# DMA issues pinned in program order, new queue times in the planner, and the output weights moved into the pattern buffers

## The chip, the cores and the metric

The kernel runs on one core of a Trainium2 chip. The metric is the time of one execution on the device, in microseconds, as the median of several executions. A profiled execution is one more execution of the same program, taken with the hardware profiler; its span runs from its first to its last instruction.

## What is computed

Two independent attention problems, A and B, share the launch; their outputs stand side by side in the last dimension. Both have 2048 rows, a model width of 512, and 32 heads of 16 channels.

```python
def _B_ref(x, wqkv, wo):
    q, k, v = ...                      # x @ wqkv, split in heads
    scores = einsum('bhqd,bhkd->bhqk', q, k) * Dh ** (-0.5)
    o = einsum('bhqk,bhkd->bhqd', softmax(scores), v)
    return o.reshape(B, S, D) @ wo

def _A_ref(x, wq, wk, wv, wo, beta):   # N = 4 segments of L = 512 rows
    for s in range(N):
        a_dot = softmax(qs @ ks^T * scale + causal mask) @ vs
        a_mem = (phi(qs) @ M) / (phi(qs) @ z + 1e-06)   # memory of earlier segments
        o = g * a_mem + (1.0 - g) * a_dot               # g = sigmoid(beta), per head
        M, z = M + phi(ks)^T @ vs, z + sum(phi(ks))     # phi(t) = t + 1 or exp(t)
    return o.reshape(B, S, D) @ wo
```

Problem B has full attention over 2048 keys, so it has by far the larger number of exponentials: 32 heads x 2048 x 2048.

## The kernel before

**Units and quads.** Heads are handled in groups. A unit is a problem, a chunk of 512 queries (`ch`), a row tile `rt` of eight heads and a half `e` of them, so four heads at a time. For one block of 128 keys (`kb`), a unit needs four score blocks of 128 x 512, one for each head of the four, made by four matmuls that use 32 rows of the array each. The exponentials of such a block go one of two ways.

- *The ScalarE way.* `scores` (L861) takes score blocks from a stream, alternately three and two at a time, into one of two PSUM tiles `s_ps`; ScalarE turns the tile of 1536 or 1024 columns into `pT` in one ACTIVATE (L882).
- *The VectorE way.* `v_scores` (L935) puts a score block into a PSUM tile `v_ps`. VectorE turns it into a half-precision bit pattern by a multiply and an add into an integer (L955, four of them for four heads). Three more integer additions over the whole pattern (L971, `v_rung`) give three shifted copies; the sum of the four approximates the exponential. All four patterns are then multiplied with V. The tiles of these patterns have the tag `vx` and `VBUFS = 11` buffers of 4 KB per partition.

Products with V are accumulated in a PSUM tile `acc` by matmuls with 32 columns each, four for a `pT` block, sixteen for a block that went the VectorE way. `zeros` matmuls (`zero`, L1103) add nothing to `acc`; they keep TensorE active.

**What sets the order.** The order is made while the program is built, by a planner written out in the kernel (L1142 to L1191). It keeps its own clocks `T["pe"]`, `T["act"]`, `T["dve"]`, `T["pool"]` and `T["sp"]`, adds constants for each operation, and picks at each step the next score tile, a V product, a chore or a filler. Chores are everything else: projections, `phi`, the memory matmuls, normalization and output projections. A chore has a due place in the stream of score blocks, and may have an `after` time or an `ok` condition. Whether a block goes the VectorE way is decided in `v_scores` and `v_pick` (L910) from VectorE's planned backlog and from `vlive`, the count of `vx` buffers in use: a new block is begun only while `vlive` is at most `VBUFS - 2`, and a copy only while it is below `VBUFS`. Compute instructions are pinned: `pin` (L96) keeps them in the order in which they were written, engine by engine. DMA issues are not pinned.

**The DMA queue.** Nearly all DMAs are issued from SyncE (SP), in one order: input weights, transposed loads of x (`load_xT`, L231), the output weights (`load_wo`, L226, called at L489 and L490), and later, in the stream, four transposing DMAs for each `phk` (L330, the transposed `phi(k)`), four for each later chunk of x, and the stores of the output (L454). The planner's `T["sp"]` is moved on by `on_sp` with 1.3 us for a transposed load of x, 1.45 us (`SPTRANS`) for a `phk` transpose and 0.55 us for a store; a projection of a newly loaded chunk is let go 3.5 us after its last issue.

**Buffers at the start.** Two weight tiles of B and three chunks of B's x occupy five of the eleven `vx` buffers at first and give them up when the last projection that reads them has been written. The two output weights have their own places in the pool `big`.

**The end.** After the last tile of the stream, L1209 to L1257 finish the last unit: transposition, reciprocal, normalization, the last output matmuls and the last stores.

A branch with an exact computation (L1367) follows; it isn't entered.

Of the kernel before, what the change touches and what calls it, by code (L numbers as in the profile page):

```python
# [13 lines left out]
BF16 = mybir.dt.bfloat16  # L14
# [6 lines left out]
P = 128  # L21
H = 32
DH = 16
D = H * DH
NRT = 4
NSEG = 4
W = 512
# [30 lines left out]
VALONE = 1.4  # L58
POOLMIN = 99
SPLOADS = 38.0  # L60
SPTRANS = 1.45
POOLTT = 1.2
POOLSLACK = -99.0
POOLWITH = 1.2
# [9 lines left out]
def kernel(  # L74
# [74 lines left out]
    def palloc(pool, shape, name):  # L149
        t = pool.tile(shape, F32, name=name, tag="misc")  # L150
        if live[0]:
            i = min(range(3), key=lambda i: slots[i])
            assert slots[i] < 1e9
            slots[i] = 1e9
            slot_of[id(t)] = (i, t)
        return t

    def on_sp(us, ready):
        T["sp"] = max(T["sp"], ready) + us
# [29 lines left out]
    rsum = const.tile([P, 64, 16], F32, name="rsum")  # L189

    def load_beta():
        nc.sync.dma_start(out=beta_a[:], in_=A_beta.partition_broadcast(P))

    def spread_beta():
        for j in range(4):
# [20 lines left out]
    def load_w(homes, name):  # L216

        t = [p.tile([P, 4, D], BF16, name=f"w_{name}", tag=tag, bufs=bufs) for p, tag, bufs in homes]
        srcs = ([B_wqkv[:, i * D:(i + 1) * D] for i in range(3)] if name == "b" else [A_wq, A_wk, A_wv])

        def load(eng, i, lo=0, hi=D):
            eng.dma_start(out=t[i][:, :, lo:hi],
                          in_=srcs[i][:, lo:hi].rearrange("(cc p) n -> p cc n", p=P))
        return t, load

    def load_wo(pool, name, eng):  # L226
        t = pool.tile([P, NRT, D], BF16, name=f"wo_{name}", tag=f"wo_{name}")
        eng.dma_start(out=t[:], in_=wos[name].rearrange("(rt p) n -> p rt n", p=P))
        return t

    def load_xT(pool, name, ch, tag, bufs):  # L231
        t = pool.tile([P, 4, W], BF16, name=f"xT_{name}", tag=tag, bufs=bufs)
        for cc in range(4):
            nc.sync.dma_start_transpose(t[:, cc, :], xs[name][ch * W:(ch + 1) * W, cc * P:(cc + 1) * P])
        return t

    def v_heads(v, kb):
# [85 lines left out]
    def do_phik(wk, k, out, then=None):  # L323

        pk = wk.tile([P, W], BF16, name="phkT", tag="phkT")

        def move():
            ph = out["ph"] = wk.tile([P, 4, P], BF16, name="phk", tag="phk", bufs=2)
            for kb in range(4):
                nc.sync.dma_start_transpose(ph[:, kb, :], pk[:, kb * P:(kb + 1) * P])  # L330
            on_sp(4 * SPTRANS, T["dve"] + 0.1)
            if then is not None:
                then()
        phase1(wk, k, pk[:], move)
        yield
# [105 lines left out]
        pin(nc.vector.tensor_reduce(okm, okt, axis=AX.X, op=ALU.min))  # L441

    def do_out(mp, wk, name, ot, wo, ch, sb, then=None):
        ps = palloc(mp, [P, D], "o_ps")
        for rt in range(NRT):
            mm(ps[:], ot[:, rt, sb * P:(sb + 1) * P], wo[:, rt, :], start=(rt == 0), stop=(rt == NRT - 1))
            if rt < NRT - 1:
                yield

        def evac():  # L450
            osb = wk.tile([P, D], BF16, name="osb", tag="osb", bufs=3)
            pin(nc.vector.tensor_copy(osb[:], ps[:]))  # L452
            r0 = ch * W + sb * P
            nc.sync.dma_start(out=out2[r0:r0 + P, col0[name]:col0[name] + D], in_=osb[:])  # L454
            on_sp(0.55, T["dve"] + 0.1)
        later(0.69, evac, ps)
        if then is not None:
            then()
# [6 lines left out]
    with ExitStack() as ms:  # L465
# [20 lines left out]
        ld(nc.sync, 0)  # L486
        ld(nc.sync, 2)
        xTB += [load_xT(wk, "b", ch, "vx", VBUFS) for ch in range(1, 4)]
        woA = load_wo(big, "a", nc.sync)  # L489
        woB = load_wo(big, "b", nc.sync)  # L490

        zeros = wk.tile([P, 1, P], BF16, name="zeros")
        nc.gpsimd.memset(zeros[:], 0.0)
# [60 lines left out]
        def seg_chores(s, rt):  # L554
            d = pos0["a", s, rt]

            def k():
                kA[s, rt] = wk.tile([P, W], BF16, name="kA", tag=f"kA{rt}")
                yield from do_k(mp, wA, xTA[s], rt, kA[s, rt][:], ("k", "a", s, rt))

            def q():
                qA[s, rt] = wk.tile([P, 2, W], BF16, name="qA", tag=f"qA{rt}")
                if s > 0:
                    phq[s, rt] = wk.tile([P, W], BF16, name="phq", tag=f"phq{rt}")
                yield from do_q(mp, wk, wA, xTA[s], rt, qA[s, rt], phq[s, rt][:] if s > 0 else None, ("q", "a", s, rt), s == 0)

            def v(kb):
                yield from do_v(mp, wA, xTA[s], kb, v_heads(vA[s], kb)[:, :, 0:DH], ("v", "a", s, kb))

            def part(g):  # L570
                yield from g
                nproj[s] = nproj.get(s, 0) + 1

            def project():
                rel = T["sp"] + 3.5
                if (s, rt) != (0, 0):
                    chore(d - LEAD, part(k()), 4, after=rel if s else ARRIVE["w1" if rt == 1 else "wk"],
                          key=("k", "a", s, rt), ok=lambda: s == 0 or ("phk", s - 1, rt) in seen)
                    chore(d - LEAD, part(q()), 4, after=rel if s else ARRIVE["w1" if rt == 1 else "wq"],
                          key=("q", "a", s, rt))  # L580
                if rt == 0:
                    for kb in range(4):
                        chore(d + 1 + 0.3 * kb, part(v(kb)), 4, after=rel if s else ARRIVE["wv"])

            def load():
                if s > 0:
                    xTA[s] = load_xT(wk, "a", s, "xTA", 1)
                    on_sp(4 * 1.3, T["pe"])
                vA[s] = wk.tile([P, 4, VROW], BF16, name="vA", tag="vA", bufs=2)
                v_ones(vA[s], 4)  # L590
                project()
                return
                yield
            if rt == 0:
                chore(d - 18, load(), 1, slot=False,
                      ok=lambda: (s < 1 or nproj.get(s - 1, 0) == 12) and (s < 2 or nmem.get(s - 2, 0) == 4))
            else:
                project()
# [34 lines left out]
        def bq_chores(ch, rt):  # L633
            qB[ch, rt] = wk.tile([P, 2, W], BF16, name="qB", tag=f"qB{rt}")

            def q():
                yield from do_q(mp, wk, wB, xTB[ch], rt, qB[ch, rt], None, ("q", "b", ch, rt))
                if rt == NRT - 1 and ch < NSEG - 1:
                    chore(pos0["b", ch, rt] - LEAD - 1.0, again(), 1, slot=False, ok=lambda: left_b[0] == 0)

            def again():
                xTB[ch + 1] = load_xT(wk, "b", ch + 1, "xTB0", 1)
                on_sp(4 * 1.3, T["pe"])
                xat[ch + 1] = T["sp"] + 3.5
                return
                yield
            chore(pos0["b", ch, rt] - LEAD - 1.5, q(), after=ARRIVE["wvb"], key=("q", "b", ch, rt),
                  ok=lambda: xat.get(ch, 1e9) < T["pe"])

        def b_kv_chores():  # L650
# [21 lines left out]
            for sb in range(S // P):  # L672
                chore(pos0["b", 0, 0] - 0.5 + 0.9 * sb, counted("v", sb // 4, g=do_v(
                    mp, wB, xTB[sb // 4], sb % 4, v_heads(VB, sb)[:, :, 0:DH], ("v", "b", sb))),
                      after=max(ARRIVE["wvb"], ARRIVE["xb"][sb // 4]))

        held.update(pk=0, ph=0)
        vlive, npool = [5], [0]

# [352 lines left out]
        def finish(u, st):  # L1032
            name, ch, rt = u["name"], u["ch"], u["rt"]
            if (name, ch) not in OT:
                assert sum(outs.get(k, 4) > 0 for k in OT) < 3
                OT[(name, ch)] = wk.tile([P, NRT, W], BF16, name=f"OT_{name}", tag="OT", bufs=3)
            ot = OT[(name, ch)]
            yield from fin_pair(wk, st, name, rt, u["sums"], ot[:, rt, :])
            if rt == NRT - 1:
                outs[name, ch] = 4  # L1040

                def gone():
                    outs[name, ch] -= 1
                at = place()
                for sb in range(4):
                    chore(at + 8 + 4 * sb, do_out(mp, wk, name, ot, woA if name == "a" else woB, ch, sb, gone))

        def v_key(q):
            u = q["u"]
# [164 lines left out]
        def partial(sb, t):  # L1214
            ps[sb] = t
            for rt in range(NRT - 1):
                mm(t, ot[:, rt, sb * P:(sb + 1) * P], woB[:, rt, :], start=(rt == 0), stop=False,
                   skip_group_check=True)
        last = [ps_s.tile([P, BANKS[(NT + i) % 2], 512], F32, name="l_ps", tag=f"s{(NT + i) % 2}") for i in range(1)]
        left = [(3, lambda: mp.tile([P, D], F32, name="l_ps3", tag="misc")[:]),  # L1220
# [14 lines left out]
        for sb in range(4):  # L1235
            pin(nc.vector.transpose(ot[:, NRT - 1, sb * P:(sb + 1) * P],
                                    tN[:, 4 * sb:4 * sb + 4, :].rearrange("p c d -> p (c d)")))
            mm(ps[sb], ot[:, NRT - 1, sb * P:(sb + 1) * P], woB[:, NRT - 1, :], start=False, stop=True,
               skip_group_check=True)
            if sb == 1:  # L1240
                fps = ps_a.tile([P, W], F32, name="f_ps", tag="misc")
# [18 lines left out]
    def exact_problem(name):  # L1260
        is_a = name == "a"
        with ExitStack() as es:
# [17 lines left out]
            w, ld = load_w([(big, f"w{i}", 1) for i in range(3)], name)  # L1280
            for i in (1, 0, 2):
                ld(nc.sync, i)
            wo = load_wo(big, name, nc.sync)
            xT = [load_xT(big, name, ch, f"xT{ch}", 1) for ch in range(4)]
            K = big.tile([P, NRT, S], BF16, name="K")
            Q = big.tile([P, NRT, 2, S], BF16, name="Q")
# [114 lines left out]
```

## Time and profile before

| | |
|---|---|
| median of 5 runs | 902.3 us (896.31 to 904.59) |
| the profiled execution's own time | 897.77 us |
| its span, first to last instruction | 896.0 us |
| ACT busy | 870.9 us (97%) |
| PE busy, with 417 filler matmuls | 865.7 us (97%) |
| DVE busy | 787.9 us (88%) |
| POOL busy | 154.2 us (17%) |
| mean granted TensorE clock | 0.995 |

Around the span lie 897.77 - 896.0 = 1.8 us. PE is TensorE, ACT ScalarE, DVE VectorE, POOL GpSimd and SP SyncE; PEld are weight loads, which overlap matmuls. A group's line gives the code line, engine, operation, the tile written and the tile read, the count, then busy time, the mean duration of one in ns, and the idle time ahead of it with what ended most of that. All matmuls are recorded at L117, so they are told apart by their tiles. Two matmuls or two ACTIVATEs in a row overlap in the records, so a group's busy time is less than count times mean.

### The profile page before, as it was taken

The page shows a single profiled execution, that of the slowest core. Times are in us where ns is not written, and L with a number is a line of the kernel's source. Part 1 is how long each engine was busy: PE and PEld are TensorE (multiplying, and loading weights), DVE is VectorE, ACT ScalarE, POOL GpSimd, SP SyncE. Part 2 cuts the span into 40 slices and gives each one's busy share as a digit, 9 for nine tenths or more (in the row PEclk, how much of TensorE's full clock was granted, in tenths as well). Part 3 has the DMA queues.
Part 4 walks back from the last instruction along what each step waited for, and adds up shares of the span by engine and source line. Part 5 has one row for each costly group of instructions (what it writes and reads, how often), then busy time and mean ns, then how long its engine had stood idle before and what let it go on. Part 6 is the DMA issues. An engine that isn't in the chain of part 4 may idle for free.

```text
span 896.0 us, 18896 instructions
## 1 busy us (share of the span) xinstructions
PE 865.7 (97%) x7649; PEld 260.2 (29%) x7649; DVE 787.9 (88%) x1348; ACT 870.9 (97%) x781; POOL 154.2 (17%) x332
## 2 busy tenths in 40 slices
PE   9999999999999999999999999999999999999996
PEld 3322222322322222222222323322232222222222
DVE  4786689888799998989889998999999998899996
ACT  6999999999999999999999999999999999999995
POOL 5710311311203022030210304002030300000000
PEclk9999999999999999999999999999999999999998
DMA  9600001100001110000000110000000000000000
GB/s 200 134 10 12 18 8 30 27 6 1 7 1 43 32 28 8 1 1 7 2 7 1 42 31 8 1 1 1 2 1 1 13 30 8 1 2 1 1 2 28
DMA packets 42800, 17.04 MB, mean 19 GB/s; under 512 B 34512, under 2 KB 42704, under 8 KB 42704
## 3 DMA queue, kind: packets, MB, share of 16 engines
q1 hardware_dynamic: 41360, 15.23, 7.4%
q8 instruction: 61, 1.00, 0.5%
q10 hardware_dynamic: 1344, 0.52, 0.2%
q14 instruction: 35, 0.29, 0.1%
HBM read 4.20 MB, written 4.19 MB: 9 GB/s over the span
## 4 chain that ended last, share of the span: by engine, by line
PE 43%; ACT 35%; issue 14%; DVE 5%; POOL 2%; ACTq 0%; DVEq 0%; POOLq 0%
ACT pT L882 34%; PE acc L117 19%; PE s_ps L117 11%; PE v_ps L117 6%; PE k_ps L117 2%; PE o_ps L117 2%; POOL pT L892 1%; DVE vx L955 1%; ACT ex L299 1%; DVE vx L971 1%; PE q_ps L117 1%; PE pre L117 1%; DVE tT L374 1%; DVE qc L272 0%; POOL qB L274 0%
## 5 line engine op out<-in xcount | busy, mean ns | idle before, releaser
L882 ACT ACTIVATE pT<-s_ps 128x1536 bf16<-128x1536 f32 x751 | 858.7, 1281 | 6.9 <-PE s_ps L117 4.6
L955 DVE TENSOR_SCALAR vx<-v_ps 128x512 uint16<-128x512 f32 x492 | 321.5, 683 | 28.4 <-PE v_ps L117 23.9
L117 PE MATMUL s_ps<-qB,KB 32*128 32x512 bf16 x1556 | 251.8, 383 | 10.8 <-ACT pT L882 7.7
L971 DVE TENSOR_SCALAR vx<-vx 128x2048 uint16<-128x2048 uint16 x369 | 242.2, 687 | 2.1 <-PE acc L117 0.8
L117 PE MATMUL acc<-vx,VB 128*32 128x512 f16 x1968 | 178.0, 385 | 1.0 <-DVE vx L955 0.7
L117 PE MATMUL v_ps<-qB,KB 32*128 32x512 bf16 x492 | 174.5, 382 | 1.5 <-DVE KB L253 0.5
L892 POOL TENSOR_SCALAR_AFFINE_SELECT pT<-pT 128x256 bf16<-128x256 bf16 (+2 forms) x240 | 104.6, 467 | 358.3 <-ACT pT L882 357.4
L117 PEld LDWEIGHTS <-KB 32*128 32x128 bf16 x2048 | 84.7, 91 | 245.6 <-issue 238.9
L117 PE MATMUL acc<-pT,VB 128*32 128x512 bf16 x1556 | 150.9, 387 | 0.3 <-DVE tT L374 0.3
L117 PE MATMUL acc<-zeros 128*128 128x512 bf16 x397 | 134.8, 387 | 0.0
L117 PEld LDWEIGHTS <-VB 128*32 128x32 bf16 x3524 | 73.6, 94 | 155.5 <-issue 144.1
L117 PEld LDWEIGHTS <-zeros 128*128 128x128 bf16 x417 | 34.2, 98 | 86.2 <-issue 80.3
L117 PE MATMUL s_ps<-qA,kA 32*128 32x128 bf16 (+3 forms) x512 | 51.4, 299 | 4.8 <-ACT pT L882 2.8
L374 DVE STREAM_TRANSPOSE tT<-acc 128x512 f32<-128x512 f32 x64 | 44.5, 700 | 12.5 <-PE acc L117 12.4
L274 POOL TENSOR_SCALAR qA<-qc,par 128x512 bf16<-128x512 bf16 x24 | 17.3, 733 | 174.8 <-DVE qc L272 174.8
L117 PE MATMUL acc<-pT,vA 128*32 128x256 bf16 (+3 forms) x512 | 32.1, 309 | 1.4 <-DVE vx L955 1.3
L117 PEld LDWEIGHTS <-kA 32*128 32x128 bf16 x512 | 17.7, 91 | 43.9 <-issue 40.9
L274 POOL TENSOR_SCALAR qB<-qc,par 128x512 bf16<-128x512 bf16 x32 | 22.6, 718 | 19.2 <-DVE qc L272 19.2
L272 DVE CAST qc<-q_ps 128x512 bf16<-128x512 f32 x28 | 19.2, 685 | 6.5 <-PE q_ps L117 5.8
L452 DVE CAST osb<-o_ps 128x512 bf16<-128x512 f32 x28 | 19.2, 684 | 5.8 <-PE o_ps L117 5.7
L408 POOL TENSOR_TENSOR tN<-tT,rsum 128x512 bf16<-128x512 f32 x1 | 1.4, 1367 | 130.9 <-DVE rsum L397 130.9
L117 PE MATMUL k_ps<-xT_b,w_b 128*128 128x512 bf16 x64 | 19.3, 383 | 0.4 <-DVE vx L955 0.2
(93 smaller groups left out, 430.7 us busy)
## 6 DMA issues: line engine op xcount, KB each, us to landing
out_dram<-osb SPq DMA_DIRECT2D x30, 128.0 KB, 1.7
w_b<-in_B_wqkv_dram SPq DMA_DIRECT2D x3, 512.0 KB, 5.1
phk<-phkT SPq DMA_TRANSPOSE x48, 2.4
w_a<-in_A_wv_dram SPq DMA_DIRECT2D x1, 512.0 KB, 4.1
wo_a<-in_A_wo_dram SPq DMA_DIRECT2D x1, 512.0 KB, 4.7
wo_b<-in_B_wo_dram SPq DMA_DIRECT2D x1, 512.0 KB, 5.6
xT_b<-in_B_x_dram SPq DMA_TRANSPOSE x28, 2.8
xT_a<-in_A_x_dram SPq DMA_TRANSPOSE x16, 2.9
```

The source lines that it names most:

```text
L117: return pin(nc.tensor.matmul(out, lhsT, rhs, **k))
L272: pin(nc.vector.tensor_copy(qc[:], ps[:]))
L274: pin(nc.gpsimd.tensor_scalar(dst[:, e, :], qc[:], par[:, e:e + 1], 0.0, ALU.mult, ALU.add))
L299: pin(nc.scalar.activation(ex[:], src, ACT.Exp))
L374: pin(nc.vector.transpose(st["tT"][:, e].rearrange("p c d -> p (c d)"), acc[:]))
L408: pin(eng.tensor_tensor(o, tT[:, :, :, 0:DH], rr.to_broadcast(bc), op=ALU.mult))
L452: pin(nc.vector.tensor_copy(osb[:], ps[:]))
L882: pin(nc.scalar.activation(pT[:, 0:n, :], pt[:, 0:n, :], ACT.Exp, scale=SCALE))
L892: pin(nc.gpsimd.affine_select(out=blk, in_=blk, compare_op=ALU.is_ge, fill=0.0, base=0, pattern=[[0, len(sls)], [1, P]], channel_multiplie ...
L955: pin(nc.vector.tensor_scalar(x[:, j, :], vt[:], XSCALE, float(LADDER[0]), ALU.mult, ALU.add))
L971: pin(nc.vector.tensor_scalar(p[:], x[:], float(off - LADDER[0]), 32767.0, ALU.add, ALU.min))
```

## The change

- Every DMA issue goes through `pin`, so DMAs keep the written order on their queue.
- The planner's times for the SP queue are larger: `SPTRANS` 1.45 to 1.5, transposed loads of x 1.3 to 1.5, a store 0.55 to 0.8, and the wait from a load's issue to its use 3.5 to 4.0.
- The output weights are no longer loaded at the start into buffers of their own. A new chore `wo_loads`, due at place 60 and allowed when two `vx` buffers are free and the stream is beyond place 40, takes two `vx` buffers, which it keeps to the end (`vlive` is raised by two and never lowered), and issues both loads. Output projections wait in the plan until 4.0 us after that.

`VBUFS` stays 11. Nothing else uses the 8 KB per partition that the pool `big` gives up.

```diff
-SPTRANS = 1.45
+SPTRANS = 1.5
...
-    def load_wo(pool, name, eng):
-        t = pool.tile([P, NRT, D], BF16, name=f"wo_{name}", tag=f"wo_{name}")
-        eng.dma_start(out=t[:], in_=wos[name].rearrange("(rt p) n -> p rt n", p=P))
+    def load_wo(pool, name, tag, bufs):
+        t = pool.tile([P, NRT, D], BF16, name=f"wo_{name}", tag=tag, bufs=bufs)
+        pin(nc.sync.dma_start(out=t[:], in_=wos[name].rearrange("(rt p) n -> p rt n", p=P)))
         return t
...
         for cc in range(4):
-            nc.sync.dma_start_transpose(t[:, cc, :], xs[name][ch * W:(ch + 1) * W, cc * P:(cc + 1) * P])
+            pin(nc.sync.dma_start_transpose(t[:, cc, :], xs[name][ch * W:(ch + 1) * W, cc * P:(cc + 1) * P]))
...
             for kb in range(4):
-                nc.sync.dma_start_transpose(ph[:, kb, :], pk[:, kb * P:(kb + 1) * P])
+                pin(nc.sync.dma_start_transpose(ph[:, kb, :], pk[:, kb * P:(kb + 1) * P]))
             on_sp(4 * SPTRANS, T["dve"] + 0.1)
...
-            nc.sync.dma_start(out=out2[r0:r0 + P, col0[name]:col0[name] + D], in_=osb[:])
-            on_sp(0.55, T["dve"] + 0.1)
+            pin(nc.sync.dma_start(out=out2[r0:r0 + P, col0[name]:col0[name] + D], in_=osb[:]))
+            on_sp(0.8, T["dve"] + 0.1)
...
-        woA = load_wo(big, "a", nc.sync)
-        woB = load_wo(big, "b", nc.sync)
+        wo = {}
...
-                rel = T["sp"] + 3.5
+                rel = T["sp"] + 4.0
...
                     xTA[s] = load_xT(wk, "a", s, "xTA", 1)
-                    on_sp(4 * 1.3, T["pe"])
+                    on_sp(4 * 1.5, T["pe"])
...
+        def wo_loads():
+            for name in "ab":
+                vlive[0] += 1
+                wo[name] = load_wo(wk, name, "vx", VBUFS)
+                on_sp(0.55, T["pe"])
+            wo["at"] = T["sp"] + 4.0
+            return
+            yield
+        chore(60, wo_loads(), 1, slot=False, ok=lambda: vlive[0] + 2 < VBUFS and place() > 40)
...
-                    chore(at + 8 + 4 * sb, do_out(mp, wk, name, ot, woA if name == "a" else woB, ch, sb, gone))
+                    chore(at + 8 + 4 * sb, do_out(mp, wk, name, ot, wo, ch, sb, gone),
+                          ok=lambda: wo.get("at", 1e9) < T["pe"])
```

The planner makes a new order from the new constants and conditions. Counted in the built programs, up to the branch that isn't entered: TensorE's order is the same up to its row 1038 (of some 15,300 with weight loads) and differs from there on.

| instructions | before | after |
|---|---|---|
| ACT, `pT` of 1536 / 1024 / 512 columns | 375 / 375 / 1 | 374 / 375 / 0 |
| DVE, first patterns (`vx` from `v_ps`) | 492 | 496 |
| DVE, shifted copies (`vx` from `vx`) | 369 | 372 |
| PE, `s_ps` from `qB` / `v_ps` from `qB` | 1556 / 492 | 1552 / 496 |
| PE, `acc` from `pT` with VB / from `vx` | 1556 / 1968 | 1552 / 1984 |
| PE, filler into `acc` | 397 | 395 |
| shifted copies that wait for a PE instruction later than DVE has waited for already | 3 | 13 |

On SP, the first four `phk` transposes now stand ahead of the chunk of A's x that followed the output weights; the output weights stand after the third `phk`, at about the 67th ACTIVATE of the stream (the first output projection of A then stands at about the 78th); all four stores of A's first chunk come after them, where three of them stood ahead of that third group of transposes before. Later, single groups of stores and transposes change places.

More of the change, by code (lines that the diff above doesn't have):

```diff
@@ L191, in load_beta @@
     def load_beta():
-        nc.sync.dma_start(out=beta_a[:], in_=A_beta.partition_broadcast(P))
+        pin(nc.sync.dma_start(out=beta_a[:], in_=A_beta.partition_broadcast(P)))
     def spread_beta():
@@ L221, in load @@
         def load(eng, i, lo=0, hi=D):
-            eng.dma_start(out=t[i][:, :, lo:hi],
-                          in_=srcs[i][:, lo:hi].rearrange("(cc p) n -> p cc n", p=P))
+            pin(eng.dma_start(out=t[i][:, :, lo:hi],
+                              in_=srcs[i][:, lo:hi].rearrange("(cc p) n -> p cc n", p=P)))
         return t, load
-    def load_wo(pool, name, eng):
-        t = pool.tile([P, NRT, D], BF16, name=f"wo_{name}", tag=f"wo_{name}")
-        eng.dma_start(out=t[:], in_=wos[name].rearrange("(rt p) n -> p rt n", p=P))
+    def load_wo(pool, name, tag, bufs):
+        t = pool.tile([P, NRT, D], BF16, name=f"wo_{name}", tag=tag, bufs=bufs)
+        pin(nc.sync.dma_start(out=t[:], in_=wos[name].rearrange("(rt p) n -> p rt n", p=P)))
         return t
@@ L443, in do_out @@
     def do_out(mp, wk, name, ot, wo, ch, sb, then=None):
+        if isinstance(wo, dict):
+            wo = wo[name]
         ps = palloc(mp, [P, D], "o_ps")
@@ L642, in again @@
                 xTB[ch + 1] = load_xT(wk, "b", ch + 1, "xTB0", 1)
-                on_sp(4 * 1.3, T["pe"])
-                xat[ch + 1] = T["sp"] + 3.5
+                on_sp(4 * 1.5, T["pe"])
+                xat[ch + 1] = T["sp"] + 4.0
                 return
@@ L1216, in partial @@
             for rt in range(NRT - 1):
-                mm(t, ot[:, rt, sb * P:(sb + 1) * P], woB[:, rt, :], start=(rt == 0), stop=False,
+                mm(t, ot[:, rt, sb * P:(sb + 1) * P], wo["b"][:, rt, :], start=(rt == 0), stop=False,
                    skip_group_check=True)
@@ L1237 @@
                                     tN[:, 4 * sb:4 * sb + 4, :].rearrange("p c d -> p (c d)")))
-            mm(ps[sb], ot[:, NRT - 1, sb * P:(sb + 1) * P], woB[:, NRT - 1, :], start=False, stop=True,
+            mm(ps[sb], ot[:, NRT - 1, sb * P:(sb + 1) * P], wo["b"][:, NRT - 1, :], start=False, stop=True,
                skip_group_check=True)
@@ L1282, in exact_problem @@
                 ld(nc.sync, i)
-            wo = load_wo(big, name, nc.sync)
+            wo = load_wo(big, name, "wo", 1)
             xT = [load_xT(big, name, ch, f"xT{ch}", 1) for ch in range(4)]
```

## Prediction

> **What bounds the kernel now.** I read the page's busy shares first, then the groups, the waits, and last a table of stretches around the one bad place.
>
> ```profile
> PE 865.7 (97%) x7649; PEld 260.2 (29%) x7649; DVE 787.9 (88%) x1348; ACT 870.9 (97%) x781; POOL 154.2 (17%) x332
> ...
> L882 ACT ACTIVATE pT<-s_ps 128x1536 bf16<-128x1536 f32 x751 | 858.7, 1281 | 6.9 <-PE s_ps L117 4.6
> L955 DVE TENSOR_SCALAR vx<-v_ps 128x512 uint16<-128x512 f32 x492 | 321.5, 683 | 28.4 <-PE v_ps L117 23.9
> ...
> L971 DVE TENSOR_SCALAR vx<-vx 128x2048 uint16<-128x2048 uint16 x369 | 242.2, 687 | 2.1 <-PE acc L117 0.8
> ```
>
> ACT is the bound: 870.9 of 896.0 us, and its main group waits only 6.9 us in all. PE's 97% is no bound, since 397 filler matmuls (134.8 us busy in their own group) are in it. DVE has 896.0 - 787.9 = 108.1 us idle. So the time is ACT's work, plus 25.1 us in which ACT is idle: at the start, at the end, and a few small gaps.
>
> The stretches split at the last exponential (columns: PE, PEld, DVE, ACT, POOL busy, then granted clock, DMA share, GB/s):
>
> ```profile
> 0.00:884.20 884.20, 861.35 (x7614) 258.77 (x7615) 783.83 (x1337) 869.80 (x779) 153.45 (x330) 1.00 0.08 19
> 884.20:896.00 11.80, 4.33 (x36) 1.39 (x34) 4.09 (x12) 1.08 (x3) 0.78 (x2) 0.77 0.17 53
> ```
>
> Of the 25.1 us, 10.7 lie in the tail and about 8.3 ahead of the first exponential (waits of 1.8, 5.6 and 0.9 us). That leaves about 6 us for the whole stream, and a third of it lies in one place:
>
> ```profile
> 388.00:392.00 4.00, 3.69 (x37) 1.20 (x37) 3.90 (x6) 4.00 (x4) 4.00 (x9) 1.00 0.00 0
> 392.00:395.60 3.60, 2.40 (x15) 0.70 (x14) 3.31 (x6) 2.99 (x4) 3.50 (x8) 1.00 0.00 0
> 395.60:399.00 3.40, 3.40 (x28) 0.86 (x30) 1.30 (x3) 2.91 (x3) 0.14 (x1) 0.50 0.00 0
> 399.00:403.00 4.00, 4.00 (x58) 1.19 (x50) 3.83 (x9) 3.02 (x4) 0.00 (x0) 1.00 0.02 4
> ```
>
> PE is slack for 3.6 us (it waits 1.29 us for DVE to empty a PSUM slot), then its clock is 0.50 for 3.4 us, and ACT starves: by its timeline it lost 0.61 + 0.33 + 0.17 + 0.97 = 2.08 us. This is the price of one clock drop.
>
> Does any compute wait for a DMA? In the waits of the whole run, after the start, only this:
>
> ```profile
> PEld L117 <- DMA w_b<-in_B_wqkv_dram: 0.3, 1, 0.3
> ```
>
> [...] The trace shows SP standing 265.7 us at stores and 186.0 us at `phk` transposes, without cost. [...] the trace has ACTIVATEs of 1450 ns.
>
> **The change, part by part.**
>
> *Pins and order on SP.* There is 0.3 us of DMA waiting in the stream to be won; worth 0. What it may cost: a transposing group takes four issues of 1.23 us (the median of `phk` issues) = 4.9 us, and 2.4 us from issue to landing, so 7.3 us. An ACTIVATE of the stream comes each (884.2 - 10.4) / 751 = 1.16 us. In the new order the tightest `phk` use stands 8 ACTIVATEs (9.3 us) behind its issue; the tightest load of x has 7 (8.1 us) for its first transpose, which needs 1.25 + 2.9. Cover is 2 us or more. Where it is gone, PE stalls by the rest, once for a segment; I take 0, bound 0 to 2 us. Pinning moves stores and `phk` transposes past each other by one group; a store's issue is 0.33 us.
>
> *Planner's queue times.* They make no instruction longer. They delay when chores may start and so deal a new order from PE's row 1038 on.
>
> *Output weights.* Two issues (0.58 and 0.51 us) leave SP at 33.2 us and come back at about the 67th ACTIVATE, 87 us. There they stand behind four transposes (4.9 us), then 0.6 us to issue and 4.7 us to land: 10.2 us. The first output matmul stands 11 ACTIVATEs later, 12.8 us. It fits with 2.6 us over; cost 0, bound 2 us if the `vx` buffer comes free late. The loads' 1 MB leave the first 50 us, but they stood behind all the loads the start needs: gain 0. The first `phk` group is issued 5.6 us earlier (the four transposes of A's x went ahead of it); nobody needs it before the 60th ACTIVATE: 0. The 16 output matmuls, 4 copies and 4 stores of A's first chunk move from 72 to 101 us to about 101 to 110 us; DVE is 76% busy from 50 to 100 us and 82% from 100 to 150 us, so they fit.
>
> *Two `vx` buffers fewer for patterns.* Thirteen shifted copies instead of three now wait for a later PE instruction. In the trace before, such waits took 0.8 and 0.3 us, so 0.55 us each: ten more are 5.5 us on DVE's queue. Behind them wait the copies that empty `v_ps`, and PE for those. DVE has 108 us idle and waits 28.4 us for `v_ps` itself, so I take 0 on the path. Bound above: each that ends in a slack PE window costs a clock drop, 2.08 us. Below 0 it can't go, a wait gives nothing.
>
> *One more block the VectorE way.* In the new order ACT has one tile of 1536 and one of 512 columns less, 2048 columns. ACT's group does 375 x 1536 + 375 x 1024 + 512 = 960,512 columns in 858.7 us, 0.894 ns each: 1.83 us. By the means of single instructions (1492 and 659 ns) it would be 2.15, but these overlap. On ACT, the bound, all of it counts: -1.8 us. DVE gets 4 x 321.5/492 + 3 x 242.2/369 = 4.6 us more, hidden by its idle time. PE gets 12 V matmuls more, 12 x 178.0/1968 = 1.1 us, and two fillers less, 0.7 us: nothing. A copy near the end could show, since DVE is 98% busy from 800 to 850 us, but over the last 50 tiles the new order has in proportion the same DVE work.
>
> *Tail.* After the last exponential the old order has V products pT, vx, vx, pT, vx, the new one pT, vx, vx, pT. One group less (four matmuls, 0.36 us): -0.3 us, bound 0 to -0.7.
>
> *Sum.* Span 896.0 - 1.8 - 0.3 = 893.9 us; the profiled execution's own time 897.8 - 2.1 = 895.7 us. That execution was 4.5 us quicker than the median of the runs; the same 2.1 us off 902.3 gives **900.2 us**.
>
> **The rivals.**
>
> *A, the sum holds: 900.2 us.* Its own range is 897.8 to 905: gaps in the stream, about 6 us, are dealt anew by the new order, by some 2 us either way, and a median of five that spread over 8.3 us may be off by 2 us.
>
> *B, the new order has fewer slack places, 896.0 us.* The median stands 4.5 us above a run with one clock drop; if drops make the difference, the median run has 1 + 4.5/2.08, about three. Two fewer: 900.2 - 4.2 = 896.0. For it: the drop sat at PE's worst wait, and its place (a segment of A ending while DVE normalizes) is reordered. Against: nothing in the change aims at it, and the number of fillers falls.
>
> *C, starved patterns, 910.6 us.* Place: from 90 us on, where two buffers are gone; a copy waits for PE's last read, the emptying of `v_ps` waits behind it, PE goes slack, and its clock drops. Price 2.08 us each. Half of the ten new waits: 900.2 + 10.4 = 910.6. It decides from four more drops on (900.2 + 8.3 = 908.5); three stay within the bound. For it: the very wait ahead of the drop was PE on DVE. Against: DVE's idle time, and the plan counts the two buffers as taken.
>
> *D, the change does nothing on the chip but move DMAs.* Then 902; it is inside A's range.
>
> **How the numbers follow.** A measurement of this kernel tells about 0.5% from no change, 4.5 us: faster is below 897.8, slower above 906.8. A (with D) 0.47, B 0.33, C 0.20. B's lower end is three drops fewer, 900.2 - 6.2 = 894.0; with the bound of the tail 893.5. The upper end, 908, takes in A with both DMA bounds (904.2) and the lower edge of C. I leave out 0.06 below and 0.14 above.
>
> **What would show it.** Right: ACT's group with 749 instructions and 856.9 us busy; no PE wait on `phk`, `wo_a` or `xT_a`; the shifted copies' idle time under 8 us; a tail of 11.1 to 11.8 us; one to three stretches at half clock. B shows as a clock mean above 0.995 and under 4 us of ACT waits in the stream; C as ACT waiting 10 us more on `s_ps`, with PE waiting on `vx` L965 ahead of each drop. A PE wait of over 2 us on a DMA would make the SP step wrong.

## The result and the profile after

| | before | after |
|---|---|---|
| median of all runs | 899.55 us (79 runs, 896.3 to 905.49) | 897.36 us (42 runs, 895.88 to 901.09) |
| ratio to before | | 0.9971, 95% interval 0.996 to 0.9982 |
| the profiled execution's own time | 897.77 us | 896.33 us |
| its span | 896.0 us | 894.6 us |

The ratio stands for a gain of 0.3%, which is under the 0.5% that the prediction called the bound of what counts. As a time, the forecast of 900.2 us was 2.8 us too high, and nearly all of that is its starting point: the 79 runs put the median of before at 899.55 us where the five runs shown first had 902.3. The prediction subtracted 2.1 us from its profile; the medians differ by 2.2 us. But the quickest runs differ by 896.3 - 895.88 = 0.4 us only. The granted clock of the single runs, recorded in steps of 0.001, tells why. These are the 83 runs of the kernel before that were timed beside e1 to e12, and 44 of the kernel after:

| mean granted clock | before: runs, mean us | after: runs, mean us | difference, us |
|---|---|---|---|
| 0.997 and 0.998 | 12, 896.4 | none | |
| 0.996 | 8, 897.5 | 5, 896.0 | -1.5 |
| 0.995 | 7, 897.7 | 11, 896.9 | -0.8 |
| 0.994 | 15, 899.3 | 7, 897.2 | -2.1 |
| 0.993 | 5, 899.7 | 13, 898.2 | -1.5 |
| 0.992 | 3, 900.3 | 3, 898.8 | -1.5 |
| 0.990 | 13, 902.0 | 2, 900.5 | -1.4 |
| 0.989 and 0.991 | none | 3, 899.1 | |
| 0.986 to 0.988 | 20, 903.9 | none | |

Within the kernel before, which is one program in one order, the time follows the clock: 0.69 us for each 0.001, by a straight line through the 83 runs (correlation 0.98). At one and the same clock the kernel after is 0.8 to 2.1 us quicker; two lines of one slope put it at 1.6 us. Its mean clock is higher, 0.9936 to 0.9923, and that is the other 0.9 us of the 2.5 us by which the means differ (900.15 and 897.67). The medians of the clock are equal, 0.994. The quickest runs are not alike: before has twelve at 0.997 or 0.998, and the kernel after has none above 0.996.

The 0.69, 1.6 and 0.9 are estimates, good to some tenths of a us: the clock counts the end of an execution too, where every profile has 2.6 to 6.0 us at half clock (5.5 in before, 2.7 in after), and the runs of before come from three chips (within 0.4 us of each other at 0.994), while the chip of those of after isn't known.

The busy row and the groups of the kernel after, as the page has them:

```profile
PE 862.8 (96%) x7659; PEld 257.9 (29%) x7659; DVE 794.6 (89%) x1355; ACT 869.1 (97%) x779; POOL 156.1 (17%) x333
...
L892 ACT ACTIVATE pT<-s_ps 128x1536 bf16<-128x1536 f32 x749 | 857.0, 1289 | 8.5 <-PE s_ps L117 6.5
L965 DVE TENSOR_SCALAR vx<-v_ps 128x512 uint16<-128x512 f32 x496 | 323.0, 682 | 28.3 <-PE v_ps L117 23.5
...
L981 DVE TENSOR_SCALAR vx<-vx 128x2048 uint16<-128x2048 uint16 x372 | 244.6, 690 | 4.5 <-PE acc L117 2.6
```

ACT's main group has two instructions fewer and is 858.7 - 857.0 = 1.7 us shorter, as summed. Its idle time went the other way, from 6.9 to 8.5 us. The idle time ahead of the shifted copies doubled, 2.1 to 4.5 us.

The stretches, split at the last exponential (columns as before):

```profile
0.00:883.02 883.02, 858.87 (x7629) 256.61 (x7629) 790.72 (x1344) 868.01 (x777) 155.32 (x331) 1.00 0.08 19
883.02:894.60 11.58, 3.97 (x32) 1.28 (x30) 3.89 (x11) 1.08 (x2) 0.78 (x2) 0.88 0.18 55
```

The tail is 11.58 us, 0.2 us less than before. I took the stream apart further by the records of the `pT` ACTIVATEs: the head ends at the first of them, the tail begins at the end of the last.

| us | before | after | difference |
|---|---|---|---|
| head | 10.40 | 9.37 | -1.03 |
| ACT busy in the stream | 867.73 | 865.94 | -1.79 |
| ACT idle in the stream | 6.07 | 7.71 | +1.64 |
| tail | 11.84 | 11.59 | -0.25 |
| span | 896.04 | 894.60 | -1.44 |

(Span here with two decimals.) In these two executions the saving of one VectorE block is there to a twentieth of a microsecond, and nearly the same amount came back as idle time of ACT. The head, which no step of the prediction counted, stands between 9.3 and 10.5 us in all the profiles of this case, and e1 below, whose order of compute is that of before, had 9.42: it isn't tied to the order.

The clock drop moved. Around it, in the kernel after:

```profile
106.00:110.30 4.30, 3.82 (x38) 1.15 (x37) 2.49 (x6) 4.30 (x5) 3.20 (x8) 1.00 0.00 0
110.30:113.70 3.40, 2.23 (x26) 0.82 (x26) 3.37 (x6) 3.40 (x4) 0.41 (x1) 0.99 0.02 5
113.70:120.50 6.80, 6.55 (x33) 1.08 (x31) 5.31 (x12) 4.98 (x5) 0.00 (x0) 0.50 0.00 0
120.50:124.00 3.50, 3.50 (x32) 1.19 (x29) 2.43 (x6) 3.25 (x3) 0.00 (x0) 1.00 0.00 0
```

PE is busy 2.23 of 3.40 us, then has half its clock for 6.8 us, and ACT is idle for 6.80 - 4.98 = 1.8 us of these. It is the picture of before at another place, 113.7 instead of 395.6 us, and twice as long. Slack on PE came ahead of it again, not a standstill. With its aftermath the drop cost ACT 0.61 + 1.43 = 2.04 us by the timeline, as much as the 2.08 of before; so the 1.64 us that ACT idled more lie elsewhere, in smaller gaps (the longest 0.7 us, at 19.4).

The order on SP, from its timeline (start, length, code line, operation, tiles, count):

```profile
50.73 35.72 SPq L330 DMA_TRANSPOSE phk<-phkT  x8
86.55 0.53 SPq L228 DMA_DIRECT2D wo_a<-in_A_wo_dram  x1
87.17 0.45 SPq L228 DMA_DIRECT2D wo_b<-in_B_wo_dram  x1
97.09 6.82 SPq L456 DMA_DIRECT2D out_dram<-osb  x4
```

The first weights were issued at 86.5 us, landed 4.1 us after that and were first read at 94.5 us. The only wait for a DMA in the list of waits is this, at the start:

```profile
POOL beta_t L197 <- DMA beta_a<-in_A_beta_dram: 7.4, 1, 7.4
```

### The profile page after: what moved, and what is told of

Its sections match the earlier page's. It is cut to its first block, busy times and chain, and to the rows that moved or that the text cites. A ratio compares the mean times of both kernels' runs of the same rounds, so it can differ in the third digit from the quotient of the medians.

```text
span 894.6 us, 18889 instructions
## 1 busy us (share of the span) xinstructions
PE 862.8 (96%) x7659; PEld 257.9 (29%) x7659; DVE 794.6 (89%) x1355; ACT 869.1 (97%) x779; POOL 156.1 (17%) x333
## 4 chain that ended last, share of the span: by engine, by line
PE 28%; ACT 15%; issue 6%; DVE 4%; POOL 1%; ACTq 0%; POOLq 0%
PE acc L117 15%; ACT pT L892 15%; PE s_ps L117 7%; PE v_ps L117 4%; DVE vx L965 1%; DVE vx L981 1%; POOL pT L902 1%; PE o_ps L117 1%; DVE tT L374 0%; PE l_ps L117 0%; PE k_ps L117 0%; ACT ex L299 0%; POOL qB L274 0%; DVE osb L1264 0%; PE q_ps L117 0%
## 5 line engine op out<-in xcount | busy, mean ns | idle before, releaser
L892 ACT ACTIVATE pT<-s_ps 128x1536 bf16<-128x1536 f32 x749 | 857.0, 1289 | 8.5 <-PE s_ps L117 6.5
L117 PE MATMUL s_ps<-qB,KB 32*128 32x512 bf16 x1552 | 252.3, 384 | 10.4 <-ACT pT L892 6.9
L117 PE MATMUL s_ps<-qA,kA 32*128 32x384 bf16 (+3 forms) x512 | 52.6, 299 | 5.0 <-ACT pT L892 2.8
L274 POOL TENSOR_SCALAR qB<-qc,par 128x512 bf16<-128x512 bf16 x32 | 23.6, 749 | 11.8 <-DVE qc L272 11.8
```

The lines of the kernel that those rows point to most:

```text
L117: return pin(nc.tensor.matmul(out, lhsT, rhs, **k))
L274: pin(nc.gpsimd.tensor_scalar(dst[:, e, :], qc[:], par[:, e:e + 1], 0.0, ALU.mult, ALU.add))
L892: pin(nc.scalar.activation(pT[:, 0:n, :], pt[:, 0:n, :], ACT.Exp, scale=SCALE))
```

## The experiments

Each kernel was timed beside the kernel before on the same chip. The theories: the *sum* says that the count of VectorE blocks sets the time and the order is worth nothing. The *clock* theory says that the time is set by clock drops, so by how the order leaves PE slack. "Fillers" are those into `acc`, as the profile has them; the expectations count those into `spare` as well (in e6 581 + 11 = 592). "Half clock" is the time at clock 0.50 inside the stream of the profiled execution. Every kernel with other constants is also a new order.

| kernel | blocks | fillers | median (lowest to highest, runs), us | ratio [95%] | half clock, us |
|---|---|---|---|---|---|
| before | 123 | 397 | 899.55 (896.3 to 905.49, 79) | | 3.4 |
| after | 124 | 395 | 897.36 (895.88 to 901.09, 42) | 0.9971 [0.996, 0.9982] | 6.8 |
| e1 | 123 | 397 | 898.85 (895.78 to 904.76, 22) | 0.9994 [0.9975, 1.0012] | 20.5 |
| e2 | 122 | 398 | 896.27 (892.46 to 900.87, 14) | 0.9955 [0.9933, 0.9978] | 6.8 |
| e3 | 122 | 412 | 898.51 (897.24 to 900.71, 22) | 0.9987 [0.9973, 1.0001] | 10.2 |
| e4 | 123 | 402 | 898.3 (897.02 to 901.46, 14) | 0.999 [0.997, 1.001] | 3.4 |
| e5 | 123 | 161 | 891.08 (889.32 to 896.41, 6) | 0.9889 [0.9849, 0.9929] | 6.8 |
| e6 | 124 | 581 | 912.36 (911.64 to 914.04, 6) | 1.0124 [1.0088, 1.0159] | none |
| e7 | 124 | 569 | 908.71 (908.05 to 911.59, 7) | 1.009 [1.0056, 1.0125] | none |
| e8 | 116 | 452 | 910.44 (910.09 to 912.78, 4) | 1.0105 [1.0057, 1.0152] | 6.8 |
| e9 | 124 | 156 | 887.58 (887.06 to 887.84, 5) | 0.9865 [0.9831, 0.9899] | none |
| e10 | 123 | 1 | 934.03 (933.82 to 934.7, 5) | 1.0383 [1.0347, 1.0419] | 171 |
| e11 | 124 | 155 | 887.66 (887.02 to 887.93, 5) | 0.9865 [0.9831, 0.9899] | none |
| e12 | 123 | 403 | 892.92 (892.79 to 893.16, 7) | 0.9928 [0.99, 0.9955] | none |

### e1: the pins alone

```diff
-nc.sync.dma_start(...)
+pin(nc.sync.dma_start(...))        # every DMA issue that the change pins; the last stores stay as they were
```

> The kernel before with every DMA pinned and nothing else. TensorE's, VectorE's and ScalarE's orders are the same as before; on SP one group of four phk transposes moves ahead of four transposed loads of x. Sum theory (time follows ScalarE's columns, 1.83 us for a block that VectorE takes): 1.000 times before, 123 blocks both. Clock theory (time follows how often TensorE's clock is halved, about 2.1 us each): also 1.000, since the slack places are the same. If pins are what makes the changed kernel faster: 0.997.

The ratio is 0.9994 (0.9975 to 1.0012): pinning is worth nothing, as forecast. Compute instructions stand in the same order as before on every engine, and on SP one group of transposes moves, so this is a second look at one order of compute, and it taught more than the pins. Its profiled execution took 904.54 us, 6.8 us more than that of before. The same stretch in both, first e1:

```profile
161.60:165.00 3.40, 2.77 (x26) 0.82 (x23) 3.40 (x6) 3.40 (x4) 1.17 (x3) 0.99 0.02 5
165.00:178.65 13.65, 12.88 (x93) 3.62 (x93) 6.64 (x15) 8.96 (x9) 6.57 (x16) 0.50 0.14 32
```

and the kernel before:

```profile
161.60:165.00 3.40, 2.75 (x26) 0.88 (x23) 3.40 (x6) 3.40 (x4) 1.17 (x3) 1.00 0.02 5
165.00:178.65 13.65, 12.72 (x133) 4.83 (x132) 9.27 (x22) 13.65 (x15) 6.95 (x17) 1.00 0.23 43
```

In the 3.4 us up to 165.0 the counts are equal on every engine. Then one keeps its clock and the other loses half of it for 13.65 us: 93 matmuls instead of 133, and ACT idle for 13.65 - 8.96 = 4.7 us instead of none. The order of the work is the same, so it alone doesn't decide. Idle time in PE's records doesn't decide it either: they cover 2.77 of the 3.40 us ahead of the drop in e1 and 2.75 of the same 3.40 us in the kernel before, which kept its clock. The two do stand differently on a grid. The half-clock stretches of one trace begin at whole steps of 3.41 us from each other: in e1 those at 165.0 and 400.5 us are 69 steps apart, in before the drop at 395.62 us and the half clock at the end, from 890.55 us, 145. So e1's grid has a border at 165.0 us, and that of before, carried back from its drop, at 163.5 and 166.9. Whether that makes the difference, no run shows. In the whole stream e1's ACT was idle for 13.39 us, in the kernel before for 6.07: 7.3 us, which covers the 6.8. At half clock e1 spent 20.5 - 3.4 = 17.1 us more, so it lost 0.40 us for each of them. The line through the 83 runs says nearly the same: 0.001 of the clock is 1.8 us at half clock, so 0.69 / 1.8 = 0.38. By this estimate a stretch of 3.41 us costs some 1.3 us, not the 2.08 that the prediction took from one place.

### e2: the planner's queue times alone

```diff
-SPTRANS = 1.45
+SPTRANS = 1.5
...
-            on_sp(0.55, T["dve"] + 0.1)
+            on_sp(0.8, T["dve"] + 0.1)
...                                    # likewise 4*1.3 to 4*1.5, and 3.5 to 4.0
```

> The kernel before with only the new queue times in the planner (1.5, 0.8, 4.0); no pins, output weights at the start. The planner gives VectorE 122 blocks instead of 123. Sum theory: 1.002 times before (+1.83 us). Clock theory: the order is dealt anew, so anything between 0.995 and 1.005, not tied to the count of blocks; the spread of the runs tells, since the kernel before spreads over 9 us and the changed one over 5 us.

The sum fails here. With one block fewer it should have been slower than before by 0.2%, and its ratio is 0.9955 (0.9933 to 0.9978); its lowest run, 892.46 us, is 3.25 us under the lowest of before beside it (895.71), both at a clock of 0.998. ACT was busy in the stream for 873.50 - 6.20 = 867.3 us, where the sum wants 867.73 + 1.79 = 869.5. Its group has one instruction more than that of before (858.7 us) and is all but as short:

```profile
L882 ACT ACTIVATE pT<-s_ps 128x1536 bf16<-128x1536 f32 x752 | 859.1, 1304 | 7.1 <-PE s_ps L117 5.4
```

Numbers that make no instruction longer moved the time by more than one block does, by the order that the planner deals from them, and not by the clock, whose mean is 0.9934 here and 0.9924 in the runs beside it (0.7 of the 4.0 us between the means).

### e3: pins and late weights, with the old queue times

```diff
-SPTRANS = 1.5
+SPTRANS = 1.45
...                                    # the other times of e2 put back as well, in the kernel after
```

> The changed kernel with the old queue times: pins and late output weights in the pattern buffers stay. 122 VectorE blocks instead of 124. Sum theory: +3.7 us against the changed kernel, so 1.001 times before with the shorter tail (0.9971 + 0.0041). Clock theory: a new deal, 0.995 to 1.005. If the late weights alone make the gain: 0.997.

The ratio is 0.9987 (0.9973 to 1.0001). The sum's 1.001 lies above the interval and the 0.997 of the late weights alone just below it. The parts don't add: e2 is 3.2 us below the median of before beside it (899.47), e3 is 1.0 below, and the whole change 2.2 below.

### e4 and e8: the kernel after, with fewer VectorE blocks

```diff
-            if vlive[0] > VBUFS - 2:
+            if vlive[0] > VBUFS - 2 or nblock[0] >= 123:      # e8: 116
...
+                nblock[0] += 1
```

> The changed kernel with VectorE's blocks capped at 123, one less than it takes; the order is the same up to the place where the 124th block would begin, near the end, so the slack places ahead of that are the same. Sum theory: +1.83 us against the changed kernel, 0.999 times before. Clock theory: the gain stays, 0.997 times before.

> The changed kernel with VectorE's blocks capped at 116, eight less than it takes. It prices a block on a longer arm: sum theory +8 x 1.83 = 14.6 us against the changed kernel, 1.013 times before. If ScalarE's columns were not what sets the end in the last part, less than half of it: below 1.006.

e4 is 898.3 - 897.36 = 0.9 us above the kernel after (its lowest run 1.1 us above), with an interval that is too wide for one block. e8 takes eight away and gives 13.1 us, 1.64 us each; ACT's busy time in the stream grew by 880.25 - 865.94 = 14.3 us, 1.79 each. ACT's group in e8:

```profile
L892 ACT ACTIVATE pT<-s_ps 128x1536 bf16<-128x1536 f32 x762 | 871.4, 1296 | 8.5 <-PE s_ps L117 6.5
```

But e8 also has 57 more fillers. At the 0.058 us for each that e6 and e9 give below, 3.3 of the 13.1 us would be theirs, which leaves 1.2 us for a block (an estimate). So ACT's share of the term "one block is 1.83 us of ACT, all of it on the path" stands to 2%; in time a block is worth less here, 0.9 us by e4 and 1.2 to 1.64 by e8.

### e5, e6, e7 and e9: more and fewer fillers

`WARMTH` is the planned activity of PE, in a window of 3 us, below which the planner inserts a filler (or takes a chore early). It was 0.52.

```diff
-WARMTH = 0.52
+WARMTH = 0.40                          # e5: after; e9: before. 0.62 in e6: before, e7: after
```

> The changed kernel with the planner's threshold for filler matmuls (WARMTH) at 0.40 instead of 0.52: 162 fillers instead of 399, and 123 VectorE blocks instead of 124. Sum theory: +1.83 us against the changed kernel for the block, nothing for the fillers, since they only take TensorE's spare time: 0.999 times before. Clock theory: TensorE is slack in more windows, its clock is halved more often, at about 2 us each: 1.005 or more, with runs spread over more than 6 us, and a profile with more than 7 us at half clock in the stream.

> The kernel before with WARMTH at 0.62: 592 fillers instead of 401 and 124 VectorE blocks (as many as in the changed kernel); no pins, old queue times, output weights at the start. Sum theory: -1.83 us for the block, 0.998 times before. Clock theory: [...] the slow runs of before (902 to 905 us) go and the median falls to its quickest runs less the block: 0.995, runs within 4 us.

> The changed kernel with WARMTH at 0.62: 580 fillers instead of 399, 124 VectorE blocks as in the changed kernel. Sum theory: as the changed kernel, 0.997 times before, or a little slower where fillers get in the way of scores. Clock theory: 0.995, runs within 4 us.

> The kernel before with WARMTH at 0.40: 156 fillers instead of 401, 124 VectorE blocks; nothing of the change in it. The changed kernel with that threshold (162 fillers, 123 blocks) took 0.989 times before, so fillers cost more than the clock drops they prevent. Filler theory: 0.987 to 0.989, a block (1.8 us) less on ScalarE, 0.2% under that run or equal to it; then nothing of the 0.989 comes from pins, queue times or late weights. If the change is what makes few fillers pay: 0.995 or more.

Both theories fail here. With 581 fillers no stretch at half clock is left in e6, and its runs lie within 2.4 us where those of before spread over 9.2, as the clock theory said; but its ratio is 1.0124 (1.0088 to 1.0159). With 156 in the kernel before (e9) the ratio is 0.9865 (0.9831 to 0.9899), and its profile shows no drop in the stream either. The kernel after goes the same way: 0.9889 with 161 fillers (e5, whose runs do spread over 7.1 us with the clock), 1.009 with 569 (e7). The chain and two groups of e6's page:

```profile
PE 84%; ACT 7%; DVE 3%; issue 3%; POOL 1%; SPq 1%; DMA 1%; ACTq 0%; DVEq 0%; POOLq 0%
...
L882 ACT ACTIVATE pT<-s_ps 128x1536 bf16<-128x1536 f32 x749 | 863.2, 1257 | 17.7 <-PE s_ps L117 10.1
...
L117 PE MATMUL acc<-zeros 128*128 128x512 bf16 x581 | 191.6, 386 | 0.0
```

and of e9's:

```profile
ACT 44%; PE 17%; issue 16%; DVE 5%; POOL 4%; DVEq 0%; ACTq 0%; POOLq 0%
...
L882 ACT ACTIVATE pT<-s_ps 128x1536 bf16<-128x1536 f32 x749 | 854.1, 1327 | 3.9 <-PE s_ps L117 2.5
...
L117 PE MATMUL acc<-zeros 128*128 128x512 bf16 x156 | 54.3, 387 | 0.0
```

Both have the same 749 ACTIVATEs. In e6 the chain of waits runs over PE for 84% of the span: PE has become the bound, by work that adds nothing. In e9 ACT leads, 44 to 17. How far ahead PE works is told by its waits for ACT to empty a score tile (total, times, longest), e6 and then e9:

```profile
PE s_ps L117 <- ACT pT L882: 1.6, 5, 0.4
```

```profile
PE s_ps L117 <- ACT pT L882: 50.0, 157, 0.8
```

Waits of PE are good news here: 157 times the next tile was wanted before ACT had let the buffer go. In e6 that was so five times. Between e6 and e9 lie 912.36 - 887.58 = 24.8 us and 581 - 156 = 425 fillers, so 0.058 us for each, at equal blocks and with no drop in either profile. A filler's record is 0.33 us (191.6 / 581), so about a sixth of it reached the end. It is no constant. The runs at a clock of 0.998 stand at 887.5 us in e9 (156), 896.4 in the kernel before (397) and 911.7 in e6 (581, one run); with 1.8 us for the block that before has less, that is 0.03 us for each filler up to 397 and 0.09 from there on. A part of each step may be the new order.

### e10: no fillers at all

```diff
-WARMTH = 0.52
+WARMTH = 0.20                          # in the kernel after
```

> The changed kernel with WARMTH at 0.20: one filler in the stream, 123 VectorE blocks. Clock theory: without fillers [...] tens of us at half clock, 1.00 times before or slower and a spread over 6 us. Filler theory carried on: each filler costs about (897.4 + 1.8 - 891.1) / 237 = 0.034 us, so 161 fewer than in the run at 0.40 give 5.5 us more, 0.983. Which of the two wins shows where fillers pay.

The other end. The granted clock in the 40 slices, and ACT's group:

```profile
PEclk9999999699776998976989698996989999999898
...
L892 ACT ACTIVATE pT<-s_ps 128x1536 bf16<-128x1536 f32 x751 | 863.1, 1305 | 39.2 <-PE s_ps L117 30.1
```

Nineteen stretches at half clock, 171 us in all, a mean clock of 0.907, and ACT waits 39.2 us. The clock theory was right on the time and wrong on the spread, which is 0.9 us; the filler theory carried on (0.983) failed. So fillers are needed: 934.03 us with one of them, 887.6 with 156, 912.4 with 581. The number that the kernel had, 397, is on the dear side of the best of these.

### e11 and e12: the two buffers given back

```diff
-VBUFS = 11
+VBUFS = 13                             # in the kernel after; e11 with WARMTH = 0.40 too
```

> The changed kernel with WARMTH at 0.40 and VBUFS at 13, which puts the two buffers back that the output weights took: 155 fillers, 124 VectorE blocks, and no shifted copy waits for a later PE instruction. Sum theory: one block off the run at 0.40, -1.8 us, 0.987. Starvation theory: more than that, 0.984 or less, since the copies' waits go too.

> The changed kernel with VBUFS at 13, threshold 0.52 as in the change: 123 VectorE blocks, 407 fillers, and no shifted copy waits for a later PE instruction (13 in the changed kernel). Sum theory: +1.8 us against the changed kernel for the block, 0.999. Starvation theory: the waits' cost goes, 0.995 or less, and VectorE's idle time ahead of the shifted copies falls from 4.5 us to below 1.

e12 is 4.4 us quicker than the kernel after, with one block fewer. The shifted copies of e12:

```profile
L981 DVE TENSOR_SCALAR vx<-vx 128x2048 uint16<-128x2048 uint16 x369 | 243.5, 692 | 1.7
```

Their idle time fell from 4.5 to 1.7 us, all of it in gaps of 0.035 us or less, so no wait is left. By the line above, some 3 of e12's 4.4 us go with the clock, 0.998 to 0.9936 in the mean. At 0.40, e11 is 3.4 us quicker than e5, with one block more; at a clock of 0.998 it is 1.7 us (887.6 to e5's one run of 889.3), which is the block. So the starvation theory has its forecast in e12 (0.995 or less) and not in e11 (0.984 or less). Both are new orders as well, so the runs don't tell what the buffers give and what the order gives. e11 and e9 are the quickest kernels of this study, both at 0.9865 (0.9831 to 0.9899); e9 has no part of the change in it.

## Why the prediction came out as it did

The forecast of a 2.1 us saving was met: 2.2 us between the medians, some 1.6 us at one clock. The 897.36 us themselves lie just below A's own range of 897.8 to 905, for the starting median was too high. Of its terms these held:

- *Pins and order on SP, 0.* Right: e1 shows no difference, and no compute in the kernel after waits for a DMA once the start is over.
- *Output weights, 0, with 2.6 us over.* Right: they landed at 86.55 + 4.1 = 90.7 us and were first read at 94.5, 3.8 us later.
- *One more block, -1.8.* Right for ACT in the profile (-1.79), though the exactness is chance: the 751 ACTIVATEs of a kernel with 123 blocks took 858.7 us in before, 857.5 in e12, 856.4 in e5 and 863.1 in e10, so one price for a column doesn't hold from order to order. In time the runs give less, 0.9 (e4) and 1.2 to 1.64 (e8).
- *Tail, -0.3.* Right, -0.25.
- *The profile's marks.* ACT's group had 749 instructions and 857.0 us against 856.9 foretold; the copies' idle time was 4.5, below 8; the tail 11.58, in its range; one stretch at half clock.

The step that was too weak is "Planner's queue times. They make no instruction longer": the prediction gave the re-dealt order no term in the sum, only "some 2 us either way" in A's range. At one clock the kernel after gained some 1.6 us where the sum has 2.1; the missing 0.5 may be its order's or the block's, the runs don't separate them. e2, e3 and e12 show how large the term can be. At one clock they stand 3.3, 0.3 and 3.2 us under the kernel before, by lines of one slope as above; the sum gives them +1.8, +1.5 (with the shorter tail) and -0.3. That leaves some 5, 2 and 3 us for the new order, in e12 with the two buffers. A term of up to some 5 us, whose sign the prediction couldn't know, stood beside a sum of 2.1 us; that it came out at 0.5 or less here is luck.

Rival B's mechanism is there, and small: the spread of one kernel's runs goes with the clock (and e1's trace shows ACT idle by as much), and the slow runs of before, 20 of 83 at 0.988 or less, have no counterpart in the kernel after. But the kernel after lost the quickest clock as well, so its mean gains 0.9 us by this and its median nothing. It also explains the lowest runs: 0.998 against 0.996 is 2 x 0.69 = 1.4 us, and with the 0.4 us that they differ this gives 1.8. The profiles without a drop in the stream (e6, e7, e9, e11, e12) are at 0.997 to 0.999, so each run of the kernel after probably had one, by the estimate above at 1.3 us. B's own marks, a clock above 0.995 and under 4 us of ACT waits, are not there: the clock is 0.995, the waits 8.5 us. And its price of 2.08 us for a drop, like C's, is half as much again as the 1.3 to 1.4 us that these runs give for one of 3.41 us.

Rival C has its waits, but not its consequence. Of the 4.5 us ahead of the copies, 2.8 are waits, 0.2 us for each of the thirteen where 0.55 was taken. They stand at 72, 74 and 399 us (0.25, 0.77 and 1.79 us), ACT lost under 0.15 us beside any of them, and the drop at 113.7 us has no such wait ahead of it. Whether two more buffers would help by another way than drops is open (e12).

A second thing was wrong without harm. "PE's 97% is no bound, since 397 filler matmuls are in it" treats a filler as free. It stands in PE's queue ahead of the next scores, and e6 and e9 show that it isn't free: the kernel before has 241 fillers more than e9 and is 899.33 - 887.58 = 11.8 us slower. At a clock of 0.998 it still is 8.8 us slower, of which at most 1.8 are a block. No drop is seen that these 241 prevent: e9's runs are at 0.998 and 0.999, those of before at 0.994 in the median.

## What to carry to other kernels

When a planner deals the order, a change of its constants is a new draw: measure the spread of draws (here some 5 us) before a sum of 2 us is believed, and count the draw as a term of the range. Where filler matmuls hold the clock up, as here, their number is a knob to be tried at both ends before anything finer (934.0 us at a clock of 0.907 with one, 887.6 at 0.998 with 156, 912.4 at 0.997 with 581), and the sign to look for is whether the producer still waits for its consumer (157 times in e9, five in e6). Compare runs at one granted clock where it is recorded: here the lowest runs, 0.998 against 0.996, hid most of the gain that the medians showed.

## What the runs showed of the hardware

- Two executions of one order of compute differed by 6.8 us, with 20.5 and 3.4 us at half clock in the stream. The 83 runs of the kernel before lie between 895.71 us at a clock of 0.998 and 904.92 at 0.986.
- The stretches at half clock in the stream lasted 3.41 us or a multiple of it (3.41 in before, 6.83 in after, 13.65 and 6.83 in e1; over all runs also 10.24, and in e10 up to 20.48), and within one execution they began on one grid of 3.41 us, the one at the end too: 395.62 and 890.55 us in before are 145 steps apart, 113.65 and 891.89 us in after 228, 165.0 and 400.5 us in e1 69. The 171 us of e10's nineteen are 50 steps. No standstill of PE came ahead of those looked at: by its records it was busy for 2.77 of 3.40 us in e1, 2.23 of 3.40 in after and 2.40 of 3.60 in before. The stretch at 161.6 us in the kernel before, 2.75 of 3.40 us busy, brought no drop, and e6 kept its clock after the window at 171.7 us, with PE busy for 1.89 of 3.40 us. So idle time in PE's records alone didn't decide. All 26 matmuls in the one at 110.3 us in after used 32 rows or 32 columns of the array; whether that counts wasn't tried.
- The busy time of the same 749 ACTIVATEs was 863.2 us in e6 and 854.1 us in e9. By shapes, e6 and then e9:

```profile
L882 ACT ACTIVATE pT<-s_ps 128x1536 bf16<-128x1536 f32 x374 | 549.8, 1470 | 17.7 <-PE s_ps L117 10.1 <-PE v_ps L117 2.0 <-ACT pT L882 0.7
L882 ACT ACTIVATE pT<-s_ps 128x1024 bf16<-128x1024 f32 x375 | 391.7, 1044 | 0.0
```

```profile
L882 ACT ACTIVATE pT<-s_ps 128x1536 bf16<-128x1536 f32 x374 | 575.1, 1538 | 3.4 <-PE s_ps L117 2.0 <-PE v_ps L117 0.4 <-ACT pT L882 0.2
L882 ACT ACTIVATE pT<-s_ps 128x1024 bf16<-128x1024 f32 x375 | 418.7, 1117 | 0.5 <-PE s_ps L117 0.5
```

The mean of one is longer in e9, 1538 to 1470 ns, and the group as a whole is shorter, 854.1 to 863.2 us. Count times mean is 994 us in e9 and 941 in e6, so the records overlap by 140 and 78 us. In the kernel before, 317 of the 364 ACTIVATEs that followed one of 1024 columns started inside its record, in the median 904 ns after its start, where the shortest records of 1024 columns last 1018 ns. In the kernel after 86% of them did so, in e9 91%, in e6 66%. The 48 of 1536 columns in the kernel before that started only after the record ahead of them had ended lasted 1450 or 1451 ns each. A start between 904 and 1018 ns comes later without idle time in the records, so the delay counts as busy time and not as a wait. Of the 24.6 us that e6's stream is longer, 14.2 are idle time and 10.4 are longer busy time; a quarter of 374 pairs at about 0.11 us each (1018 - 904 ns) would be 10.3 (an estimate).
